# Keys of the first tile in two steps, two more tiles turned on TensorE, and a new written-out order, in a two-layer linear-attention and gated-MLP kernel

## The chip, the cores and the metric

One core of one Trainium2 chip runs the whole program in one launch. The metric is the device time of one execution in microseconds; lower is better. PE is TensorE's matmul stream and PEld its weight loads, DVE is VectorE, ACT is ScalarE, POOL is GpSimd, SP is the engine whose queue issues most of the DMAs.

## The reference

The input x has 2048 rows (tokens) of 512 in bf16. Two layers follow each other; both use the same weights. Each layer adds an attention step and then an MLP step to x, each on a layernorm of x:

```python
def _A_ref(x, wqkv, w_phi, wo):            # H = 32 heads of Dh = 16
    q, k, v = ...                          # from x @ wqkv, split by heads
    pq = einsum("bhsd,hdf->bhsf", q, w_phi)
    pk = einsum("bhsd,hdf->bhsf", k, w_phi)
    phi_q = concat([softmax(pq), softmax(-pq)])
    phi_k = concat([softmax(pk), softmax(-pk)])
    kv = einsum("bhsf,bhsd->bhfd", phi_k, v)
    z  = einsum("bhsf->bhf", phi_k)
    num = einsum("bhqf,bhfd->bhqd", phi_q, kv)
    den = einsum("bhqf,bhf->bhq", phi_q, z) + 1e-6
    return (num / den) @ wo
def _B_ref(x, W_gate, W_up, W_down):       # F = 1376
    gate = x @ W_gate; up = x @ W_up
    return (gate * (gate > 0) * up) @ W_down

x = x + _A_ref(layernorm(x)); x = x + _B_ref(layernorm(x))   # and once more
```

The attention is linear: kv and z are sums over all tokens, so that no query of a layer can be finished before the last key of that layer.

## The kernel before

The tokens are 16 tiles of 128 rows. For each tile of a layer the work is, in order:

- `norm_A`: mean and variance of the tile (DVE, "stats" and "aggr"), `ln` and `rstd` on ACT (rsA), then x scaled to xn (on DVE, or on POOL, there with a small instruction for the negated mean nm before it).
- `turn`: xn is transposed into xnTA. One way is by PE: four transposes of 128 columns against the identity into a PSUM bank, then a copy out by ACT or DVE. The other is one DMA on SP's queue for two tiles at once ("pair"). In the first layer tiles below `PAIRN` go by PE, the others by DMA as pairs; `PAIRN` is 4 before.
- Keys: `Keys.begin` multiplies xnTA with Wk2, takes two exponentials (ek, on ACT, of the value and of its negative), multiplies xnTA with wv (V), copies V into vext, and sums ek on DVE (sk). `finish` and `scale` turn the sums into a factor (ln and exp on ACT) and scale ek in two halves (DVE or POOL). `kvz` adds ek times vext into one PSUM bank over all 16 tiles.
- Queries: `query` multiplies xnTA with Wq2, takes exponentials and sums, scales, and turns the result by DMA (fq).
- `build` makes R from the sums; `attend` multiplies fq with R (erq), divides, turns (oT), and projects with wo; `mlp` does the gated MLP for blocks of one to four tiles.

Wk2 and Wq2 are folded weights: `fold` multiplies the weight with `Wblk`, the block-diagonal form of w_phi with its mean taken off, so that one matmul gives k times w_phi. For that the weight must be turned first: wk by PE (16 transposes of 128 columns into four PSUM banks, copied out to SBUF by ACT or DVE), then for each of four row blocks four matmuls of 128 columns with Wblk (16 in all), and four copies into Wk2. Wq's weight is turned by four DMAs on SP, its 16 fold matmuls go between the first tiles. So a tile's first key needs wk, w_phi (wf), Wblk and all four copies of Wk2; wk lies in a tile that is named hT in the traces, because the MLP uses it later.

Every step is an `op(engine, cost, due, emit, ...)`. The list of ops is made by the loops above; then `arrange` takes each op's order, buffer and engine from written-out tables: `ORDER` is the order of emission (an op's number is its place of creation), `SLOTS` the buffer that each op takes, `PLACE` one digit for each op that has an alternative engine. Each engine runs its instructions in that order and waits at the first that isn't ready. There are six PSUM banks (p_b) for nearly everything on PE and one more for kvz and erq. PE begins with nine matmuls on zeros ("warm"), which compute nothing.

DMA issues share eight semaphores in turn, so that the ninth issue waits for the first to land, the tenth for the second, and so on.

Of the kernel before, what the change touches and what calls it, by code (L numbers as in the profile page):

```python
# [8 lines left out]
P = 128  # L9
# [4 lines left out]
NB = D // P  # L14
NF = 11
FR = F - (NF - 1) * P
T = 16
# [82 lines left out]
def mm(n, cols):  # L100
    t = n * (cols / 2.4 + 2.5)
    return t, t + 170, n
# [40 lines left out]
class K:  # L143
# [9 lines left out]
    "0101111100101100001010011011110000100001111011010110111000001101011001000010110000111010010000010000"  # L153
    "0010010100000001111001111010110011000001111000110110011110001111000101001001000110110000100010000111"
    "0011010011011011000001110101110010000101010010000001001000100010001000001010110001101101010111000011"
    "010000110000000001101011110100010011100001110011101111"
)
SLOTS = (
    "0011542321002200002341032141012103362101231434404125j4422i5312281024c0330125132k00002b0004951314g423"
    "1e41205354370055313a222d131f04582546001b163h300034130124130c2521320706391100050401151502000225011020"  # L160
    "0500001114010022350210003100001155021002001401004000015205125e33102414110214302510310g04000200200152"
    "2215403520252225221j21311041130411310211252130152021002440102353051383314b2000464022f043001410305001"
    "301310400211321121324501222511005434101040159521003032121131131255132033021422h2124c2012020032050152"
    "0422331141155k313015i13215200i034a242k351d265e115d120f13360053054504583237263j2122131a30010401021414"
    "0000124402100044010001340210124302000043011021240110400025211311121001130410105001200503212211011001"
    "3525524313500042000002141022155020245231052132214003203540112501511114520122403101512101402105022135"
    "000200110411442140220243214113013120412210500400541032135"
# [7 lines left out]
PAIRN, PAIRK, READY = 4, T, (2, 3)  # L175
# [100 lines left out]
def kernel(  # L276
    ctx: ExitStack, tc: tile.TileContext, A_x, A_wqkv, A_w_phi, A_wo, B_x, B_W_gate, B_W_up,
    B_W_down, out):
    nc = tc.nc
# [529 lines left out]
    xT = []  # L809
# [101 lines left out]
```

## Time and profile before

| | us |
|---|---|
| median of 3 runs | 373.67 (373.5 to 373.74) |
| the profiled execution's own time | 373.55 |
| its span | 371.8 |
| PE busy | 363.0 (98%) |
| DVE busy | 266.9 (72%) |
| ACT busy | 209.3 (56%) |
| POOL busy | 99.8 (27%) |

A row of a timeline gives the start, the length, the engine and line, the operation with its shapes, how many of them in a row, and in brackets the idle time before it and what ended it. Matmuls are pipelined: one of 512 columns shows as 379 ns though the next starts 216 ns later, so that times on PE are best taken from start to start. A row of the DMA view gives the issue, its size and the time from issue to landing. Shares of busy time are means over stages with different limits.

### The profile page before, as it was taken

How to read it: one execution, taken by the hardware profiler on the slowest of the kernel's cores; microseconds unless marked ns; L12 is line 12 of the kernel's file. 1: busy time of each engine (PE TensorE's matmuls, PEld its weight loads, DVE VectorE, ACT ScalarE, POOL GpSimd, SP SyncE). 2: the span in 40 equal slices, each digit the busy share in tenths (PEclk: the TensorE clock that was granted, in tenths of full speed). 3: DMA queues.
4: the chain of work that ended last, by engine and by line, in shares of the span. 5: the costliest groups of instructions: out<-in, count | busy, mean ns of one | idle time of the engine just before them, and what ended most of it. 6: DMA issues, size and time to landing. Idle time of an engine off the chain costs nothing.

```text
span 371.8 us, 7423 instructions
## 1 busy us (share of the span) xinstructions
PE 363.0 (98%) x2786; PEld 216.4 (58%) x2828; DVE 266.9 (72%) x562; ACT 209.3 (56%) x575; POOL 99.8 (27%) x126
## 2 busy tenths in 40 slices
PE   8899999999999999999999999999999999999996
PEld 4445557776555545455567555687664544457764
DVE  6899999999797573846899887998668362433343
ACT  5989999473644772454554768775343426313111
POOL 4799863350220100003621184252100000000000
PEclk9999999999999999999999999999999999999999
DMA  8869838777516050131134000359754302010033
GB/s 220 190 153 193 278 84 154 112 146 144 111 23 119 2 100 2 29 71 37 28 65 85 3 0 3 58 94 170 151 77 72 51 14 30 0 43 15 9 118 104
DMA packets 93443, 31.20 MB, mean 84 GB/s; under 512 B 85376, under 2 KB 92384, under 8 KB 93408
## 3 DMA queue, kind: packets, MB, share of 16 engines
q1 hardware_dynamic: 92736, 30.59, 40.5%
q8 instruction: 22, 0.36, 0.4%
q10 hardware_dynamic: 672, 0.15, 0.2%
q14 instruction: 13, 0.11, 0.1%
HBM read 7.91 MB, written 2.10 MB: 27 GB/s over the span
## 4 chain that ended last, share of the span: by engine, by line
PE 91%; DMA 3%; ACT 2%; DVE 2%; issue 1%; POOL 0%; DVEq 0%; POOLq 0%
PE b L754 36%; PE b L794 19%; PE b L617 7%; PE b L561 7%; PE b L555 6%; PE b L677 6%; PE b L730 3%; PE q L590 2%; PE q L654 2%; DMA xnTB<-xn 1%; DMA xnTA<-xn 1%; PE q L430 1%; PE b L480 1%; ACT ek L558 1%; DVE X L681 1%
## 5 line engine op out<-in xcount | busy, mean ns | idle before, releaser
L754 PE MATMUL b<-xnTB,wgu 128*128 128x128 bf16 (+2 forms) x1200 | 153.3, 279 | 0.3 <-DMA xnTB<-xn 0.3
L754 PEld LDWEIGHTS <-wgu 128*128 128x128 bf16 x1200 | 97.6, 98 | 47.5 <-DMA xnTB<-xn 0.4
L758 ACT ACTIVATE gu<-b 128x512 bf16<-128x512 f32 (+1 forms) x83 | 47.1, 580 | 70.3 <-PE b L754 64.6
L794 PE MATMUL b<-wd,hT 128*128 128x512 bf16 (+3 forms) x346 | 84.5, 372 | 0.8
L529 POOL TENSOR_TENSOR ek<-ek,sk 128x512 bf16<-128x512 bf16 x47 | 51.2, 1115 | 93.3 <-ACT sk L578 93.3
L794 PEld LDWEIGHTS <-hT 128*128 128x128 bf16 (+1 forms) x363 | 34.3, 98 | 34.1 <-DVE hT L762 0.3
L771 DVE TENSOR_TENSOR hT<-gu,b 128x512 bf16<-128x512 bf16 (+1 forms) x40 | 26.0, 657 | 24.8 <-ACT gu L758 18.7
L566 DVE TENSOR_REDUCE sk<-ek 128x64 f32<-128x1024 bf16 x32 | 38.1, 1207 | 7.9 <-ACT ek L558 7.8
L623 DVE TENSOR_REDUCE sq<-ek 128x64 f32<-128x1024 bf16 x32 | 38.5, 1209 | 6.2 <-ACT ek L620 6.2
L558 ACT ACTIVATE ek<-b 128x512 bf16<-128x512 f32 x64 | 36.4, 607 | 10.0 <-PE b L555 9.0
L638 POOL TENSOR_TENSOR ek<-ek,sq 128x512 bf16<-128x512 bf16 x28 | 30.5, 1094 | 34.5 <-DVE sq L634 23.6
L620 ACT ACTIVATE ek<-b 128x512 bf16<-128x512 f32 x64 | 36.5, 608 | 3.7 <-PE b L617 3.7
L801 DVE SCALAR_TENSOR_TENSOR X<-b,rsB,X 128x512 bf16<-128x512 f32 (+2 forms) x33 | 23.7, 729 | 20.4 <-PE b L794 20.4
L677 PE MATMUL b<-wo,oT 128*128 128x512 bf16 x121 | 32.1, 379 | 0.4
L555 PE MATMUL b<-Wk,xnTA 128*128 128x512 bf16 x119 | 31.2, 379 | 1.3 <-DMA xnTA<-xn 0.8
L561 PE MATMUL b<-wv,xnTA 128*128 128x512 bf16 x128 | 32.2, 379 | 0.1
L773 ACT CAST gu<-b 128x512 bf16<-128x512 f32 (+1 forms) x43 | 24.6, 575 | 13.5 <-PE b L754 10.8
L617 PE MATMUL b<-Wq,xnTA 128*128 128x512 bf16 x119 | 30.7, 379 | 0.3
L762 DVE TENSOR_TENSOR hT<-gu 128x512 bf16<-128x512 bf16 (+1 forms) x43 | 21.7, 511 | 11.9 <-ACT gu L773 11.9
L681 DVE SCALAR_TENSOR_TENSOR X<-b,X 128x512 bf16<-128x512 f32 x32 | 21.7, 683 | 9.5 <-PE b L677 9.1
L668 DVE TENSOR_TENSOR o<-q,rd 128x512 bf16<-128x512 f32 x32 | 22.0, 688 | 3.2 <-ACT rd L665 2.6
L490 DVE BATCH_NORM_STATS2 bstA<-X 128x6 f32<-128x512 bf16 x32 | 21.7, 685 | 2.9 <-DMA X<-in_A_x_dram 2.6
(80 smaller groups left out, 349.1 us busy)
## 6 DMA issues: line engine op xcount, KB each, us to landing
out_dram<-X SPq DMA_DIRECT2D x15, 128.0 KB, 1.8
X<-in_A_x_dram SPq DMA_DIRECT2D x6, 256.0 KB, 4.1
wgu<-in_B_W_up_dram SPq DMA_DIRECT2D x4, 344.0 KB, 4.5
wgu<-in_B_W_gate_dram SPq DMA_DIRECT2D x4, 344.0 KB, 4.7
wd<-in_B_W_down_dram SPq DMA_DIRECT2D x5, 256.0 KB, 5.5
hT<-in_A_wqkv_dram SPq DMA_DIRECT2D x2, 256.0 KB, 3.8
wv<-in_A_wqkv_dram SPq DMA_DIRECT2D x2, 256.0 KB, 4.4
wo<-in_A_wo_dram SPq DMA_DIRECT2D x4, 128.0 KB, 4.2
```

Source lines behind the costliest of these rows:

```text
L529: e.tensor_tensor(out=out().rearrange("p g s (h f) -> p (g s h) f", f=DH)[:, lo:lo + n], in0=ek.t[:].rearrange("p g s (h f) -> p (g s h) f ...
L555: k = op("PE", mm(4, 512), due, lambda: [nc.tensor.matmul(kp.t[:], lhsT=xnTA[c][:, i, b, :], rhs=Wk2[:, b, :], start=(b == 0), stop=(b == ...
L558: e = [op("ACT", act(512), due, lambda s=s: nc.scalar.activation(out=ek.t[:, :, s, :], in_=kp.t[:].rearrange("p (g e) -> p g e", e=GQ), fu ...
L561: v = op("PE", mm(4, 512), due_v, lambda: [nc.tensor.matmul(vp.t[:], lhsT=xnTA[c][:, i, b, :], rhs=wv[:, b, :], start=(b == 0), stop=(b == ...
L566: a = op("DVE", SUM16, due, lambda: nc.vector.tensor_reduce(out=sk.t[:, row, :], in_=ek.t[:].rearrange("p g s (h f) -> p (g s h) f", f=DH) ...
L617: q = op("PE", mm(4, 512), due, lambda: [nc.tensor.matmul(qp.t[:], lhsT=xnTA[c][:, i, b, :], rhs=Wq2[:, b, :], start=(b == 0), stop=(b == ...
L620: e = [op("ACT", act(512), due, lambda s=s: nc.scalar.activation(out=ek.t[:, :, s, :], in_=qp.t[:].rearrange("p (g e) -> p g e", e=GQ), fu ...
L623: a = op("DVE", SUM16, due, lambda: nc.vector.tensor_reduce(out=sq.t[:], in_=ek.t[:].rearrange("p g s (h f) -> p (g s h) f", f=DH), axis=A ...
L677: a = op("PE", mm(4, 512), due + 3, lambda j=j, yp=yp: [nc.tensor.matmul(yp.t[:], lhsT=oT.t[:, j, b, :], rhs=wo[:, b, :], start=(b == 0), ...
L754: nc.tensor.matmul(ps.t[:, q * W:(q + 1) * W].rearrange("p (i t) -> p i t", t=P), lhsT=wgu[:, s, b, g * P:(g + 1) * P], rhs=xT.t[:, 0:n, b ...
L758: nc.scalar.activation(out=gu.t[:, 0, 0:cols], in_=gp.t[:, 0:cols], func=AF.Relu)
L794: nc.tensor.matmul(yp.t[:, 0:c1 - c0], lhsT=h.t[:m, f * W + i * P:f * W + (i + 1) * P], rhs=wd[:m, f, c0:c1], start=(f == 0), stop=(f == N ...
```

## The change

Three things change.

First, tile 0's keys in the first layer no longer use Wk2. With `PLAIN = 1`, the tile's xnTA is multiplied by wk itself as it was loaded: 16 matmuls of 128 columns give the keys in turned form (name "KT"), one copy brings them from PSUM to SBUF (kT, in a buffer of the pool gu), and four matmuls of 128 columns with Wblk give what Wk2 gave. So this tile waits for wk and Wblk but not for the turned wk, its folds and the four copies. The other tiles use Wk2 as before.

Second, `PAIRN` goes from 4 to 6: tiles 4 and 5 of the first layer are turned on PE, each by four transposes and a copy, no longer by a DMA as a pair, and their ln and rsA are taken for each by itself.

Third, `ORDER`, `SLOTS` and `PLACE` are new tables. The op numbers shift by seven, as there are seven more ops. From about the 890th of 1,888 entries the order is the old one but for small swaps. In the first part much moves:

- SP's queue before begins: first half of wk, tiles 2 and 1 of x, second half of wk, tiles 8 and 9, tile 3, a turned block of Wq, tiles 4 and 5, half of wv, tiles 6 and 7, half of wv, three turned blocks of Wq, the turned pair 4 and 5. After it begins: wf (before on ACT's queue), tile 2, wk's two halves, tile 3, tiles 4 and 5, tiles 12 and 13, wv's two halves, tiles 8 and 9, a turned block of Wq, tiles 6 and 7, tile 1, a turned block, tiles 10 and 11, two turned blocks, the turned pair 12 and 13.
- PE before turns all of wk with the first folds between, then tiles 0 to 3, and begins the keys of three tiles. After it turns half of wk, tile 0, a quarter of wk, does a fold, the last quarter, a fold, KT, two folds, turns two tiles, does the second step of tile 0's keys, the values of two tiles, a fold of Wq, and then the first key by Wk2. The first key of a tile turned by DMA (tile 12) comes after eight groups of K and V by 512 columns and all folds of Wq.
- By `PLACE`, in the first part: one Wq copy and one copy of the turned wk go from DVE to ACT, the kT copy is on ACT, three of the copies of turned tiles go to DVE; tile 0's scaling goes from POOL to DVE; in the phi halves two go from POOL to DVE; three of the reciprocals of `attend` go from ACT (as ln and exp) to DVE.

```diff
@@ -150,21 +150,21 @@
 PLACE = (
-    "0101111100101100001010011011110000100001111011010110111000001101011001000010110000111010010000010000"
...
+    "0100100000101001000110111111111000110001101100000010110110100001100111000100110110110101000000000000"
...
 SLOTS = (
...
@@ -172,103 +172,104 @@
 SUM_ON_PE, SPLIT = False, False
-PAIRN, PAIRK, READY = 4, T, (2, 3)
+PAIRN, PAIRK, READY = 6, T, (2, 3)
+PLAIN = 1
...
 ORDER = (
-    16, 0, 3, 17, 30, 22, 24, 25, 8, 4, 26, 18, 19, 7, 1, 12, 47, 9, 323, 27, 48, 31, 28, 20, 2, 49, 33, 83, 50, 10,
...
+    16, 0, 4, 17, 30, 23, 18, 8, 19, 24, 20, 26, 22, 3, 21, 1, 9, 47, 10, 27, 48, 14, 85, 28, 2, 49, 50, 6, 31, 86, 51,
...
@@ -552,9 +553,20 @@
             c, i = t // C, t % C
             kp, vp = Buf(p_a), Buf(p_b)
             ek, vx = Buf(p_ek), Buf(p_v)
-            k = op("PE", mm(4, 512), due, lambda: [nc.tensor.matmul(
-                kp.t[:], lhsT=xnTA[c][:, i, b, :], rhs=Wk2[:, b, :], start=(b == 0), stop=(b == NB - 1))
-                for b in range(NB)], [xT] + k_fold, [kp], name="K")
+            if self.l == 0 and t < PLAIN:
+                kT, tp = Buf(p_gu), Buf(p_b)
+                k = op("PE", (960, 1130, 16), due, lambda: [nc.tensor.matmul(
+                    tp.t[:, e * P:(e + 1) * P], lhsT=wk[:, b, e * P:(e + 1) * P], rhs=xnTA[c][:, i, b, :],
+                    start=(b == 0), stop=(b == NB - 1)) for e in range(NB) for b in range(NB)],
+                    [xT] + l_wk, [tp], name="KT")
+                k = evac("DVE", due, lambda: kT.t[:, 0, :], lambda: tp.t[:], [k], [kT], [tp], "kT")
+                k = op("PE", mm(4, 128), due, lambda: [nc.tensor.matmul(
+                    kp.t[:, b * P:(b + 1) * P], lhsT=kT.t[:, 0, b * P:(b + 1) * P], rhs=Wblk[:, b, :],
+                    start=True, stop=True) for b in range(NB)], [k, c_blk], [kp], [kT], name="K")
+            else:
+                k = op("PE", mm(4, 512), due, lambda: [nc.tensor.matmul(
+                    kp.t[:], lhsT=xnTA[c][:, i, b, :], rhs=Wk2[:, b, :], start=(b == 0), stop=(b == NB - 1))
+                    for b in range(NB)], [xT] + k_fold, [kp], name="K")
```

More of the change, by code (lines that the diff above doesn't have):

```diff
@@ L152 @@
 PLACE = (
-    "0101111100101100001010011011110000100001111011010110111000001101011001000010110000111010010000010000"
-    "0010010100000001111001111010110011000001111000110110011110001111000101001001000110110000100010000111"
-    "0011010011011011000001110101110010000101010010000001001000100010001000001010110001101101010111000011"
-    "010000110000000001101011110100010011100001110011101111"
+    "0100100000101001000110111111111000110001101100000010110110100001100111000100110110110101000000000000"
@@ L157 @@
+    "1010001100011000100100000011010110110000001111000010000011010001111001011100001010110110000100010000"
+    "1110011010011011011000001110101110010000101010010000001001000100010001000001010110001101101010111000"
+    "011010000110000000001101011110100010011100001110011101111"
 )
 SLOTS = (
-    "0011542321002200002341032141012103362101231434404125j4422i5312281024c0330125132k00002b0004951314g423"
-    "1e41205354370055313a222d131f04582546001b163h300034130124130c2521320706391100050401151502000225011020"
@@ L161 @@
[L161 to L165, printed above, removed]
@@ L166 @@
-    "3525524313500042000002141022155020245231052132214003203540112501511114520122403101512101402105022135"
-    "000200110411442140220243214113013120412210500400541032135"
+    "000135042302101020000338141155200220314111214223023342022e0001g23115b4402a53312j2020i013226311554320"
+    "3d5211c01210442490047113f121k234h34111555260e30463302061c211814343550024a002321000305011313020002240"
+    "110201200001153000020340210121000101133020000220504002102521300513d24102511115211211103402b130100002"
+    "2023013021253105114g3230740201251110321242511231001431230421552030231230212405541125e5134h1322005101"
@@ new lines @@
+    "0320012010252240011001021532041430012362301013103332018212114111012013302422224051424035441010400210"
+    "310342541220050033j20220390432i0449135f264j350k203d113k121h132e043c055i0631322a2027214g130f340115200"
+    "2051500101055020002550110012502001052021002520100214501025001031012110111100225020030001013224044011"
+    "1112123133152023211510210041500440332411531202340241052121123510113013100153110145220203040205240231"
+    "14023120400000500551052442452115112212011504400300520350121023"
```

178 rows, old and new, of the table ORDER are left out of this document.

## The prediction

> **What bounds the kernel now.** I read the page's busy line first, then the stretches (busy time by window), then PE's timeline of the first 22 us, then ACT, POOL and the DMA issues beside it.
>
> ```profile
> PE 363.0 (98%) x2786; PEld 216.4 (58%) x2828; DVE 266.9 (72%) x562; ACT 209.3 (56%) x575; POOL 99.8 (27%) x126
> 5.03:18.47 13.44, 11.85 (x97) 7.09 (x96) 12.25 (x32) 12.52 (x37) 10.20 (x20) 1.00 0.90 217
> 18.47:54.00 35.53, 35.20 (x271) 18.33 (x278) 34.63 (x50) 34.15 (x101) 30.77 (x35) 1.00 0.76 182
> 54.00:100.00 46.00, 45.63 (x469) 32.05 (x473) 43.99 (x95) 29.07 (x94) 14.19 (x21) 1.00 0.71 132
> 20.00:30.00 10.00, 9.95 (x61) 4.80 (x61) 10.00 (x19) 9.97 (x30) 9.38 (x13) 1.00 0.67 173
> ```
>
> The columns are length, then PE, PEld, DVE, ACT and POOL busy. PE is the bound of the whole: after 18.47 it is idle for 0.33 us of 35.53, then 0.37 of 46. Only the start loses. So any change to this kernel is worth two things: PE work added, and PE time lost before 18.47. But between 18.47 and 54 ACT and DVE are nearly as full as PE, so that work put on them there has no idle time to go into.
>
> PE's timeline of the start (start, length, line, count, idle before):
>
> ```profile
> 1.19 4.02 PE L430 MATMUL q<-zero 128*128 128x512 bf16 x9 [1.19 <-DVE zero L397]
> 5.00 1.06 PE L454 MATMUL b<-ident,hT 128*128 128x128 bf16 x8
> 6.35 0.79 PE L462 MATMUL b<-Wblk,hT 128*128 128x128 bf16 x8 [0.29 <-POOL Wblk L416]
> 6.97 0.61 PE L454 MATMUL b<-ident,hT 128*128 128x128 bf16 x8
> 9.45 0.40 PE L480 MATMUL b<-ident,xn 128*128 128x128 bf16 x4 [0.40 <-POOL xn L512]
> 9.69 2.75 PE L555 MATMUL b<-Wk,xnTA 128*128 128x512 bf16 x11
> 14.23 0.39 PE L462 MATMUL b<-Wblk,hT 128*128 128x128 bf16 x4
> 14.45 1.03 PE L561 MATMUL b<-wv,xnTA 128*128 128x512 bf16 x4
> 17.30 0.39 PE L462 MATMUL b<-Wblk,hT 128*128 128x128 bf16 x4
> 18.47 1.90 PE L555 MATMUL b<-Wk,xnTA 128*128 128x512 bf16 x7 [0.78 <-DMA xnTA<-xn]
> 20.20 1.03 PE L561 MATMUL b<-wv,xnTA 128*128 128x512 bf16 x4
> 21.07 1.03 PE L617 MATMUL b<-Wq,xnTA 128*128 128x512 bf16 x4
> ```
>
> Lengths overlap, so I price by starts. Four matmuls of 512 columns take 21.07 - 20.20 = 0.87; four of 128 columns 14.45 - 14.23 = 0.22. From the end of the nine warm-up matmuls (5.03) to 18.47 the order of before runs 64 matmuls of 128 columns (16 to turn wk, 16 folds of Wk, 16 folds of Wq, four tiles turned by four) and 32 of 512 (K and V four times each): 16 x 0.22 + 8 x 0.87 = 10.5 us of work in 13.44. So the start loses 2.9 us, the last piece of it in the wait for the first pair of tiles turned by DMA. The new order must take more from these 2.9 us than the change adds.
>
> **PE work added.** Tile 0's K was four matmuls of 512 (0.87). It becomes sixteen of 128 with the plain wk and four of 128 with Wblk: 5 x 0.22 = 1.10, so 0.23 more. Tiles 4 and 5 turned on PE are eight of 128: 0.44. Together 0.67 us, and none of it is hidden unless PE would otherwise wait, which it does only in the start.
>
> **The new start, step by step.** The rows that price it:
>
> ```profile
> 4.68 0.22 DVE L411 TENSOR_REDUCE cmean<-wf 128x4 f32<-128x64 bf16 x1 [0.54 <-DMA wf<-in_A_w_phi_dram]
> 5.25 1.05 POOL L416 TENSOR_TENSOR Wblk<-wf,Mf 128x512 bf16<-128x512 bf16 x1 [3.94 <-DVE vext L399]
> 8.62 0.77 POOL L512 TENSOR_SCALAR xn<-X,nm,rsA 128x512 bf16<-128x512 bf16 x1
> 9.37 0.19 POOL L510 TENSOR_SCALAR nm<-mvA 128x1 f32<-128x1 f32 x1
> 11.91 0.32 ACT L498 ACTIVATE lnA<-mvA,eps 128x2 f32<-128x2 f32 x1
> 12.36 1.07 ACT L558 ACTIVATE ek<-b 128x512 bf16<-128x512 f32 x2
> 13.32 0.30 ACT L498 ACTIVATE lnA<-mvA,eps 128x2 f32<-128x2 f32 x1
> 7.92 1.54 ACT L436 CAST Wk<-b 128x512 bf16<-128x512 f32 x3
> 9.34 0.32 ACT L498 ACTIVATE lnA<-mvA,eps 128x1 f32<-128x1 f32 x1
> 10.95 1.09 ACT L558 ACTIVATE ek<-b 128x512 bf16<-128x512 f32 x2
> wf<-in_A_w_phi_dram ACTq DMA_DIRECT2D x1, 16.0 KB, 3.5
> hT<-in_A_wqkv_dram SPq DMA_DIRECT2D x1, 256.0 KB, 3.3
> hT<-in_A_wqkv_dram SPq DMA_DIRECT2D x1, 256.0 KB, 4.3
> 0.74 0.44 SPq L348 DMA_DIRECT2D hT<-in_A_wqkv_dram  x1
> 7.25 3.81 SPq L449 DMA_TRANSPOSE hT<-in_A_wqkv_dram  x3
> ```
>
> An ACT pass over 512 columns costs 0.48 (two ek from 12.36 to 13.32, three casts from 7.92 to 9.34), an ln with its rsA 0.45 (11.91 to 12.36), a tile scaled on POOL 1.04 (xn at 8.62, its successor's nm at 9.37 and 0.29 more).
>
> Loads. On SP's queue wf now goes first (0.74) and the first half of wk third, behind wf and one tile of x: at somewhat under 0.5 an issue, at about 1.7 rather than 0.74. wf lands 0.74 + 3.5 = 4.24 instead of 4.68, so Wblk is ready near 5.85 instead of 6.30. wk's first half lands at 1.7 + 3.3 = 5.0 at best, and at 1.7 + 4.3 = 6.0 at worst. Bytes queued ahead of it are fewer than ahead of the 4.3 row, so I take 5.1: PE's first turn starts about where it does now.
>
> Tile 0. Its scaling moves from POOL, where it stands behind Wblk, to DVE: statistics, one ln and rsA, and the scaled tile is there near 5.8. PE turns it behind the first eight of wk (until about 6.4), ACT copies it by 7.1, the sixteen matmuls with wk run until about 8.1. ACT must then finish two casts before kT, so the second step runs near 9.1, 0.6 earlier than PE's first K now (9.69).
>
> ACT, the chain that decides. From 8.0 on its new queue holds four casts (Wk, kT, Wk, Wk: 1.9), two ln and two rsA (0.6, half overlapped), a fourth Wk cast, a vext, an ln: tile 0's first exp stands at 8.0 + 1.9 + 0.6 + 0.96 + 0.2 = 11.7, where now it runs at 10.95. So the two-step key does not bring tile 0's exponentials forward; it only gives PE work while ACT is busy. Up to the next wait on a DMA there follow on ACT rsA, vext, three ek, ln, ek, ln, rsA, Wq, rsA, ek, Wq, a key sum's ln, vext, ek: with that first exp eleven passes of 0.48 and 0.9 of small ones, to 17.9. The bank for PE's first K of a DMA-turned tile (tile 12) is then free: PE reaches it at 18.05.
>
> POOL and the pair. POOL scales tiles 2 and 3, then 4 and 5, then the pair 12 and 13. Tile 4 needs an rsA that stands behind those four casts (10.6); the four end at 10.6 + 0.77 + 3 x 1.04 = 14.5. SP is free by then: the transposes of Wq's weights take 1.27 of issue each, and a later start and the loads between them move the last one's end from 11.1 to about 12.3. So the pair is issued at about 14.5, against 13.57 now for the first pair. Its landing:
>
> ```profile
> 13.57 1.23 SPq L475 DMA_TRANSPOSE xnTA<-xn  x1
> xnTA<-xn SPq DMA_TRANSPOSE x1, 4.9
> xnTA<-xn SPq DMA_TRANSPOSE x1, 4.6
> xnTA<-xn SPq DMA_TRANSPOSE x1, 3.4
> X<-in_A_x_dram SPq DMA_DIRECT2D x1, 256.0 KB, 4.1
> ```
>
> These are the first three pairs of before (issued at 13.57, 16.05, 19.17) and a load of x beside the first. The new pair has loads issued right behind it, like the first two, so I take 4.6: landed at 19.1, with 17.9 and 19.4 as ends. The load row is for a transfer of the same 256 KB. The Trainium skill ("Advanced Engine Details and Errata", X-Bar Transpose) says that transposing DMAs are as fast as regular ones; two of three rows here are slower than that load, one faster. By that rule the pair would land at 14.5 + 4.1 = 18.6 and the result would be 0.5 lower than mine.
>
> Sum. Up to this wait the new order has run 88 matmuls of 128 (16 turning wk, five tiles, 16 + 16 folds, 20 for tile 0's K) and 32 of 512: 22 x 0.22 + 8 x 0.87 = 11.8. From 5.03 to 19.1 are 14.07, so the start loses 2.3 against 2.9: 0.6 won. PE's added work takes 0.67. Net +0.07 us, which is nothing. The ends: landing at 17.9 leaves PE's own arrival, 18.05, a loss of 1.2, and the net is 1.7 - 0.67 = 1.0 won; landing at 19.4 gives 2.6 and 0.4 lost.
>
> Behind the start. The order written out is the same but for a shifted numbering and small swaps in its later half, so what counts is 19 to 54. There PE has no slack and I cost the new order at nothing. The cover is ACT's lead: K's and Q's exponentials lag PE by banks. If that cover is gone, see the second rival. DVE gets three more copies of turned tiles, one scaling and two halves of phi, and gives up a Wq cast and a copy of wk's turned weights; the copies stand in its start, where it has 1.2 us idle (13.44 - 12.25). POOL is relieved of a tile and two halves. Of the moved work, one pair fewer on SP (1.23 of issue) frees a queue that nobody waits for.
>
> Against the profiled execution: 373.55 for a span of 371.8, and the median 373.67. 373.55 + 0.07 is 373.6, which I give as the time.
>
> **The rivals.** A measurement of this kernel can tell about 0.2%, 0.75 us, from no change.
>
> Faster: the pair lands like the third one (3.4) and PE never waits; then 1.0 us comes off, 372.6. For it: nothing else is in the transposing queue then. Against it: the two pairs with the same neighbours took 4.6 and 4.9. It can hardly give more, since PE's own arrival hangs on ACT. Chance 0.27.
>
> Slower, by ACT: by the new order's list ACT gets one Wq cast, the kT cast and one more copy of wk's turned weights, one xnTA copy less, and one ln with rsA more (two singles for one pair): 2 x 0.48 + 0.45 = 1.4 us before 54, while it has 1.4 us idle there now (35.53 - 34.15), 0.91 of it one gap:
>
> ```profile
> 19.54 1.09 ACT L558 ACTIVATE ek<-b 128x512 bf16<-128x512 f32 x2 [0.91 <-remote]
> ```
>
> That line is where ACT waited for the keys of the first pair. It decides as soon as PE waits for a bank between 20 and 50: then the 1.4 us arrive on PE whole, 373.6 + 1.4 = 375.0. Against it: three pairs of ln and exp for the denominators go to DVE near 55. Chance 0.22.
>
> Slower, by a late full rate: nine 512-column matmuls of the warm-up took 4.02, 0.43 each against 0.22 later, and the first eight of 128 took 1.06 against 0.61 for the second eight, though the granted clock reads 1.00 throughout. So the array runs at half rate until about 6. If PE pauses for wk at 5.03 and the half rate lasts until 9, the ten groups of 128 that stand between (2.2 us) take 4.4, of which 0.8 falls into waits; ACT, POOL and the pair come 1.4 later: 375.0. The Trainium skill ("TensorE: Matmul & The Clock Gate", Parts 1 and 4) has the array at half rate until some 3.4 us of sustained work and does not count transposes as work, and the new order puts sixteen of them ahead of its first fold where before has eight. The trace agrees on the half rate; that transposes don't count it does not show. Chance 0.08.
>
> Nothing of the start is won: the new start loses 2.9 as the old one does, and only the added work remains, 374.3. Chance 0.10; it is no change by the bound.
>
> **How the numbers follow.** The forecast has 0.33. No change within 0.2% is 372.92 to 374.42: 0.33 + 0.10 = 0.43. Faster 0.27, slower 0.22 + 0.08 = 0.30. The forecast's own range is 372.9 to 374.1. The range to hold 8 in 10 goes from 372.5 to 375.0: it takes in the faster case and the ACT case, and leaves out mixes of the two slower cases.
>
> **What would show it.** Right: tile 0's second step near 9.1, tile 0's first ek near 11.7, the first xnTA pair issued near 14.5, and PE idle 0.5 to 1.4 us before the K that follows, the only DMA wait on PE up to 54. Wrong: the first turn of wk starting after 5.6; PE waiting for banks (idle ended by ACT) between 20 and 54; PE past that K by 18.2; or a PE busy sum that grew by other than 0.7.

## The result, and the profile after

| | before | after |
|---|---|---|
| median of 6 runs, us | 373.47 (373.21 to 373.74) | 375.81 (374.99 to 376.04) |
| the profiled execution's own time | 373.55 | 376.04 |
| its span | 371.8 | 374.2 |
| its last matmul starts | 368.05 | 370.61 |

The change makes the kernel slower: the ratio of the times is 1.006 [1.005, 1.007], 2.3 us. The prediction was 373.6 in 372.5 to 375.0; the time lies above the range.

Busy time by stretch in the changed kernel (length, then PE, PEld, DVE, ACT, POOL, granted clock, DMA share, GB/s):

```profile
5.03:18.47 13.44, 11.94 (x114) 7.70 (x115) 11.76 (x28) 12.01 (x35) 8.06 (x19) 1.00 0.96 223
18.47:54.00 35.53, 35.36 (x283) 18.54 (x282) 35.09 (x46) 35.02 (x105) 32.33 (x35) 1.00 0.69 175
54.00:100.00 46.00, 44.97 (x475) 31.71 (x474) 39.94 (x96) 27.11 (x83) 12.87 (x18) 1.00 0.72 129
```

Against the same rows of before, the start and the stretch up to 54 look no worse. PE's idle time between 54 and 100 has grown from 0.37 to 1.03. DVE's idle time between 18.47 and 54 has shrunk from 0.90 to 0.44. What PE waited for (total, times, longest):

```profile
PE b L567 <- DMA xnTA<-xn: 1.3, 1, 1.3
PE q L431 <- DVE zero L398: 1.2, 1, 1.2
PE b L573 <- DMA wv<-in_A_wqkv_dram: 0.9, 1, 0.9
PE b L455 <- POOL nm L511: 0.8, 1, 0.8
PE q L666 <- DVE R L619: 0.6, 1, 0.6
PE b L481 <- DVE o L680: 0.3, 1, 0.3
PE b L573 <- ACT ek L632: 0.2, 1, 0.2
```

The wait for zero opens the warm-up, as before. The row with nm is the first turn of the key weights, at 5.52; what it waited for is rather their first half, which landed at 5.47. The first line is the largest new one, and PE's timeline puts it in the second layer, in a part of the order that the change left as it was:

```profile
10.58 1.90 PE L573 MATMUL b<-wv,xnTA 128*128 128x512 bf16 x8 [0.94 <-DMA wv<-in_A_wqkv_dram]
55.38 0.41 PE L666 MATMUL q<-R,fq 128*128 128x68 bf16 x8 [0.63 <-DVE R L619]
56.97 0.40 PE L481 MATMUL b<-ident,o 128*128 128x128 bf16 x4 [0.31 <-DVE o L680]
206.88 1.90 PE L567 MATMUL b<-Wk,xnTA 128*128 128x512 bf16 x8 [1.29 <-DMA xnTA<-xn]
```

To find all of the 2.56 us by which the last matmul starts later, I took the start of each matmul in the trace and subtracted what the matmuls before it cost back to back (512 columns 0.216 us, 256 0.109, 128 0.056). In the trace of before 42 matmul records are missing, each put in at its cost. What is left over is time lost:

| stretch, us | lost before | lost after | difference |
|---|---|---|---|
| 1.5 to 30 | 4.86 | 3.91 | -0.95 |
| 30 to 54 | 0.20 | 0.31 | +0.11 |
| 54 to 60 | 0.08 | 1.28 | +1.20 |
| 60 to 200 | 0.30 | 0.71 | +0.41 |
| 200 to 250 | -0.08 | 1.59 | +1.67 |
| 250 to 300 | 0.66 | 0.08 | -0.58 |
| work added on PE | | | +0.70 |

The lines add to 2.56. So there are two losses to explain, 1.20 behind the last key product and 1.67 in the second layer, and two gains, 0.95 in the start and 0.58 near 271.

For the second layer, the DMA view in two windows of 3.1 us, each from the issue of the same pair of tiles on. First before, then after:

```profile
q1 hardware_dynamic: 1056, 0.26, 44.1%
xnTA<-xn SPq DMA_TRANSPOSE x1, 3.0
```

```profile
q1 hardware_dynamic: 1046, 0.26, 44.0%
q8 instruction: 1, 0.02, 1.9%
xnTA<-xn SPq DMA_TRANSPOSE x1, 4.6
```

The pair carries the same bytes, but in the changed kernel one packet of the queue "instruction" moves beside it, and the pair lands after 4.6 us instead of 3.0. Over the whole execution that queue moves 22 packets of 16 KB:

```profile
q8 instruction: 22, 0.36, 0.4%
```

PE runs 2852 matmuls and as many weight loads, so one packet goes with some 260 of its instructions. The packets' times in the trace follow PE's program: 60 empty instructions on PE move the one at 208.5 to 202.7 (e1, below). The change adds 24 pairs of weight load and matmul near the start. The work at 202 us thus moved by 1.5 us, and the packet, counted in pairs, came earlier against it: 208.5 us before, 7.8 behind the issue of this pair; 204.7 after, 2.5 behind it. The theory, then, is that the packet in its flight makes the pair late, and the first experiments test it. Its rival was that the late landing came of the new order or of chance.

### The profile page after: what moved, and what is told of

Read it like the earlier page. It is cut to its first block, busy times and chain, and to the rows that moved or that the text cites. A ratio compares the mean times of both kernels' runs of the same rounds, so it can differ in the third digit from the quotient of the medians.

```text
span 374.2 us, 7496 instructions
## 1 busy us (share of the span) xinstructions
PE 365.3 (98%) x2852; PEld 216.9 (58%) x2852; DVE 268.7 (72%) x568; ACT 209.8 (56%) x574; POOL 97.2 (26%) x122
## 4 chain that ended last, share of the span: by engine, by line
PE 79%; ACT 9%; DVE 6%; DMA 3%; issue 1%; SPq 1%; DVEq 0%
PE b L766 35%; PE b L806 19%; PE b L689 7%; PE b L629 4%; ACT ek L570 4%; PE b L573 3%; PE b L567 3%; PE b L742 3%; PE q L666 2%; DVE ek L530 2%; DMA X<-in_A_x_dram 1%; ACT ek L632 1%; DVE sk L578 1%; ACT vext L437 1%; DMA xnTA<-xn 1%
## 5 line engine op out<-in xcount | busy, mean ns | idle before, releaser
L806 PE MATMUL b<-wd,hT 128*128 128x512 bf16 (+3 forms) x363 | 86.2, 373 | 0.0
L530 POOL TENSOR_TENSOR ek<-ek,sk 128x512 bf16<-128x512 bf16 x45 | 50.3, 1140 | 56.4 <-ACT sk L590 55.2
L570 ACT ACTIVATE ek<-b 128x512 bf16<-128x512 f32 x64 | 36.4, 621 | 7.5 <-PE b L567 7.5
L632 ACT ACTIVATE ek<-b 128x512 bf16<-128x512 f32 x64 | 35.5, 615 | 6.7 <-PE b L629 6.7
L629 PE MATMUL b<-Wq,xnTA 128*128 128x512 bf16 x128 | 32.2, 379 | 0.0
L774 DVE TENSOR_TENSOR hT<-gu 128x512 bf16<-128x512 bf16 (+1 forms) x43 | 20.6, 484 | 12.0 <-ACT gu L785 12.0
```

Source lines behind the costliest of these rows:

```text
L530: e.tensor_tensor(out=out().rearrange("p g s (h f) -> p (g s h) f", f=DH)[:, lo:lo + n], in0=ek.t[:].rearrange("p g s (h f) -> p (g s h) f ...
L570: e = [op("ACT", act(512), due, lambda s=s: nc.scalar.activation(out=ek.t[:, :, s, :], in_=kp.t[:].rearrange("p (g e) -> p g e", e=GQ), fu ...
L629: q = op("PE", mm(4, 512), due, lambda: [nc.tensor.matmul(qp.t[:], lhsT=xnTA[c][:, i, b, :], rhs=Wq2[:, b, :], start=(b == 0), stop=(b == ...
L632: e = [op("ACT", act(512), due, lambda s=s: nc.scalar.activation(out=ek.t[:, :, s, :], in_=qp.t[:].rearrange("p (g e) -> p g e", e=GQ), fu ...
L806: nc.tensor.matmul(yp.t[:, 0:c1 - c0], lhsT=h.t[:m, f * W + i * P:f * W + (i + 1) * P], rhs=wd[:m, f, c0:c1], start=(f == 0), stop=(f == N ...
```

## The experiments

Each was measured against the kernel before on the same chip; the runs were spread over four chips, on which the kernel before took 373.52 to 373.61. e6, e8, e11 and e12 carry e2's empty instructions too, and e7, e8 and e9 some of their own, to keep the packets where they do no harm. The last two columns come from the profiled execution: when PE's first numerator product starts (it needs R, so it stands for everything up to R), and how long PE takes from there to its last matmul.

| run | median, us | ratio to before | first numerator | from there to the end |
|---|---|---|---|---|
| before | 373.47 | | 53.85 | 314.20 |
| after | 375.81 | 1.006 [1.005, 1.007] | 55.38 | 315.23 |
| e1_shift_before | 375.47 | 1.0045 [1.0033, 1.0057] | 53.81 | 316.46 |
| e2_shift_after | 373.95 | 1.0012 [1.0003, 1.0021] | 55.39 | 313.74 |
| e3_cover | 376.00 | 1.0065 [1.0053, 1.0077] | 55.01 | 315.48 |
| e4_both | 374.04 | 1.0017 [1.0004, 1.0030] | 57.39 | 313.84 |
| e5_before_clear | 372.94 | 0.9987 [0.9978, 0.9996] | 53.70 | 313.74 |
| e6_mask_early | 373.35 | 1.0003 [0.9990, 1.0016] | 54.89 | 313.38 |
| e7_pair_by_dma | 379.31 | 1.0143 [1.0126, 1.0161] | 59.92 | 314.09 |
| e8_one_step_keys | 374.77 | 1.0041 [1.0024, 1.0057] | 56.02 | 313.41 |
| e9_turn_alone | 373.21 | 0.9991 [0.9982, 1.0000] | 54.02 | 313.72 |
| e10_before_clear2 | 373.37 | 0.9995 [0.9986, 1.0004] | 54.17 | 313.79 |
| e11_ek_early | 374.36 | 1.0029 [1.0017, 1.0042] | 55.23 | 313.49 |
| e12_ek_and_mask | 373.74 | 1.0004 [0.9995, 1.0012] | 54.80 | 313.52 |

**e1 and e2: move the packet, nothing else.** The means is an empty instruction on PE. It does no work, but it takes a place in PE's program, so that every packet behind it comes earlier against the work. Before and after get a few of them where PE's sequencer runs ahead of the array:

```diff
             if o.eng == "PE":
                 idle(next(fill, 0))
             o.emit()
+            if o.eng == "PE":
+                for _ in range(NOPS.get(pe, 0)):
+                    nc.tensor.nop("pad")
+                pe += 1
+NOPS = {k: 6 for k in range(256, 266)}     # e1, in the kernel before
+NOPS = {k: 7 for k in range(256, 266)}     # e2, in the changed kernel
```

> The kernel before with 60 empty instructions in TensorE's program, six behind each of ten of its steps between about 190 and 197 us, so that its instruction packet of 16 KB that moved at 208.5 us comes 30 pairs of weight load and matmul earlier, at about 203. Theory 1 (such a packet that falls into the flight of a transposing DMA lengthens it): the pair issued near 200.7 us lands after 4.6 to 4.9 us and not 3.04, its K waits about 1.3 us near 205.5, and the time is 374.4 to 375.0 against 373.5. Theory 2 (the late landing in the changed kernel comes of its other order, or of chance): the pair lands after about 3.05 us and the time stays 373.4 to 373.7. If the empty instructions themselves cost, TensorE shows gaps between 190 and 197 us; expected is under 0.2 us.

> The changed kernel with 70 empty instructions in TensorE's program, seven behind each of ten of its steps between about 189 and 197 us, so that its instruction packet that moved at 204.7 us comes 35 pairs earlier, at about 200.4, ahead of the pair that is issued at 202.2. Theory 1 (packet in the flight lengthens it): that pair lands after about 3.05 us and not 4.63, the wait of 1.3 us at 206.9 is gone, and the time is 374.4 to 374.8 against 375.8. Theory 2: the pair still lands after 4.6 us, and the time stays at 375.8, or rises by what the empty instructions cost.

The DMA view over 3.1 us from the issue of the pair, in e1 (the kernel before with the packet moved into the flight):

```profile
q8 instruction: 1, 0.02, 1.8%
xnTA<-xn SPq DMA_TRANSPOSE x1, 4.4
```

and in e2 (the changed kernel with the packet moved out of it; no such line of the queue is there):

```profile
q1 hardware_dynamic: 1056, 0.26, 44.1%
xnTA<-xn SPq DMA_TRANSPOSE x1, 3.1
```

The same edit makes the one kernel slower by 1.95 and the other faster by 1.86. In e2 the wait is gone and PE loses 0.13 between 200 and 250 instead of 1.59. In e1 PE waits where it never did, and at a second place, which the expectation did not have:

```profile
205.11 1.25 PE L555 MATMUL b<-Wk,xnTA 128*128 128x512 bf16 x5 [1.03 <-DMA xnTA<-xn]
287.02 1.04 PE L677 MATMUL b<-wo,oT 128*128 128x512 bf16 x4 [1.35 <-ACT gu L773]
```

The second is again a packet (at 282.7) in the flight of a pair of oT, issued at 281.67, that landed after 5.3 us; the row names ACT, which had long been done. Both kernels' gaps between 190 and 200 us stayed as they were, so the empty instructions cost nothing there. Theory 1 stands: the landings came as it had them, in both directions. The times went further than it had them, e1 over its 375.0 by the second place, and e2 under its 374.4: of e2's 1.86 the profiled executions show 1.5, and for the rest I have no place.

**e3 and e4: give PE something to do while it waits for R.** Two Q groups move ahead, on PE alone:

```diff
- PE's part of ORDER: ... Q470, erq488, Q443, oT492, erq496, Q407 ...
+ PE's part of ORDER: ... Q470, Q443, erq488, Q407, oT492, erq496 ...
```

> The changed kernel with two steps of its written-out order moved on TensorE alone: the Q group that stood behind the first numerator product now stands ahead of it, and the next Q group stands ahead of the first turn of o. Theory 1 (the 1.2 us that TensorE loses between 54 and 60 us is the wait for R on VectorE with too little to do meanwhile): the waits of 0.63 for R and 0.31 for o shrink to 0.2 together, and the time falls by 0.6 to 1.1 us, to 374.7 to 375.2. Theory 2 (VectorE and ScalarE are late by as much in what follows, and the wait only moves): the gaps reappear between 57 and 75 us, and the time stays within 0.3 us of 375.8.

> The changed kernel with both edits, the two Q groups moved and the 70 empty instructions. If the two losses are separate, the gains add: 1.0 to 1.4 for the packet and 0.6 to 1.1 for the cover, 373.3 to 374.2 us, level with the kernel before (373.5) within 0.7. If the new order loses by something else as well, or the cover is given back, it stays over 374.4.

In e3 the wait for R is gone, and two others stand in its place, behind R in the same chain:

```profile
56.60 0.40 PE L481 MATMUL b<-ident,o 128*128 128x128 bf16 x4 [0.31 <-DVE o L680]
57.68 1.04 PE L689 MATMUL b<-wo,oT 128*128 128x512 bf16 x4 [0.42 <-ACT oT L437]
```

PE lost 1.27 us between 54 and 60, against 1.28. e4, with the packet cleared as well, is 0.1 from e2, which lacks the move, so that its 374.04 lies in the range for two gains by the packet's alone. Theory 2 had the time and the waits behind R right: a Q group moved ahead fills the wait for R and is then missing in the chain from R to the first projection. e4's profiled execution took 376.66, 2.6 over its median; the last section says why.

**e6, e11 and e12: why R is late.** VectorE around R (start, length, operation) before, and after:

```profile
49.03 0.57 DVE L424 TENSOR_TENSOR Mg<-Mf 128x4 f32<-128x4 f32 x1
53.01 0.69 DVE L602 TENSOR_TENSOR R<-q,Mg 128x512 bf16<-128x512 f32 x1 [0.29 <-PE q L590]
53.71 1.21 DVE L623 TENSOR_REDUCE sq<-ek 128x64 f32<-128x1024 bf16 x1
```

```profile
52.49 1.01 DVE L425 TENSOR_TENSOR Mg<-Mf 128x4 f32<-128x4 f32 x1
53.43 1.21 DVE L635 TENSOR_REDUCE sq<-ek 128x64 f32<-128x1024 bf16 x1
54.55 0.67 DVE L614 TENSOR_TENSOR R<-q,Mg 128x512 bf16<-128x512 f32 x1
```

Before, VectorE stands idle when the last key product ends (52.97) and takes R at once. After, it has no idle time: the last key product ends at 53.88, and a sum that stands behind the mask keeps VectorE until R at 54.55. So R is 1.55 later: 0.91 because PE itself comes to its last key product later, with one Q group (0.87) more ahead of it, and 0.64 on VectorE, which takes 0.67 from there to R where it took 0.04. e6 moves the mask to where VectorE waits for x. Each line shows the part of one engine, VectorE for the mask and ScalarE for ek:

```diff
 ORDER: ... 38, 121 (stats), 260 ...   ->  ... 38, 121, 29 (Mg), 260 ...      # e6, e12
 ORDER: ... 42 (W2), 142 (ln) ...      ->  ... 42, 57, 58 (ek of tile 0), 142 ...   # e11, e12
```

> The changed kernel with the 70 empty instructions of the run before (packet clear of the pair at 202 us) and one VectorE step moved in the written-out order: the 1.0 us that spreads the mask Mg, which stood two steps ahead of R at 52.5 us, goes to 8.3 us, where VectorE waits for x. Theory 1 (the 1.2 us between 54 and 60 us come of VectorE, which is 2.2 us behind with Mg and a sum when the last key product ends): R starts at about 53.9 and not 54.55, what TensorE loses there falls from 1.28 to 0.2 to 0.5 us, and the time is 372.9 to 373.4 against 373.95 without the move. Theory 2 (the chain behind R is as late as R, as moving Q groups showed, so the loss moves on): 373.7 to 374.1.

> The changed kernel with the 70 empty instructions that clear the pair at 202 us, and one move on ScalarE in the written-out order: tile 0's two exponentials, which stood behind the value copy and began at 12.5 us, stand right behind the third copy of the folded weights, at about 9.9, where ScalarE waited 0.77 us. In every run so far R started 41.4 to 42.2 us after the first exponential of keys, with ScalarE busy for 97 to 99 per cent of that and VectorE for 99. Theory A (ScalarE's stream sets R): R starts 0.5 to 0.8 us earlier than 54.55, and the time is 373.1 to 373.5 against 373.95 without the move. Theory B (VectorE's stream sets R): R stays within 0.2 of 54.55, and the time at 373.8 to 374.1.

> The run beside it with the mask Mg moved to 8.3 us on VectorE as well. Theory A alone: as the run beside it, 373.1 to 373.5. Theory B alone: as the mask alone, R at about 54.05 and 373.2 to 373.5. Both streams near their bound: R at 53.3 to 53.7, what TensorE loses between 54 and 60 us falls under 0.5, and the time is 372.5 to 373.1, under the kernel before.

VectorE in e6:

```profile
52.63 1.21 DVE L635 TENSOR_REDUCE sq<-ek 128x64 f32<-128x1024 bf16 x1
54.05 0.69 DVE L614 TENSOR_TENSOR R<-q,Mg 128x512 bf16<-128x512 f32 x1 [0.22 <-PE q L602]
```

VectorE is now ahead of the last key product, which ends at 54.01, and waits 0.22 for it. R starts 0.5 earlier, PE's loss between 54 and 60 falls from 1.28 to 0.65, and the time from 373.95 to 373.35. The time lies in Theory 1's range; the loss does not, it was to fall to 0.2 to 0.5. Theory 1 had VectorE 2.2 behind, and it was 0.67. What is left lies behind R, where the wait of 0.31 for o stays. (The intervals of the ratios of e2 and e6 overlap, so that the 0.6 of time is less sure than the rows.) In e11 tile 0's first exponential starts at 9.91 instead of 12.53, and R comes no earlier than this:

```profile
54.41 0.67 DVE L614 TENSOR_TENSOR R<-q,Mg 128x512 bf16<-128x512 f32 x1
```

R is 0.15 earlier than in e2, within the 0.2 of Theory B. So ScalarE's stream does not set R, and Theory A falls. The regularity that had led me to it (42 us from the first exponential to R in nearly every run) was a coincidence of starts: in e11 it is 44.5. e12 repeats e6 (R at 53.96). The medians of e11 and e12 are each 0.4 above the kernel without the earlier exponentials (374.36 against e2's 373.95, 373.74 against e6's 373.35), above the ranges of both theories, and I have no place for that: the profiled execution of e11 took less than that of e2 (374.19, 374.58).

**e5 and e10: clear the packets in the kernel before.** Empty instructions only, dealt out in two ways (in short):

```diff
+NOPS = {0: 42, and 5 behind each of ten steps at 211 to 220 us}     # e5
+NOPS = {0: 36, and 6 or 5 behind each of the same ten}              # e10
```

> The kernel before, nothing of its work changed, with 42 empty instructions behind its warm-up products, where TensorE waits for weights anyway, and 50 more in ten of its steps between about 211 and 220 us. Its packets of 16 KB of instructions then come 21 pairs of weight load and matmul earlier (the one at 16.4 us at about 13.2), and 46 pairs earlier from 220 us on (the one at 269.4 at about 262.5). Theory 1 (a packet in the flight lengthens a transposing DMA): the first pair of normalised tiles, issued at 13.6 us, lands after 3.1 to 3.5 us and not 4.85, the wait of 0.7 to 0.8 us at 18.5 is gone, so is that of 0.3 at 271.5, and the time is 372.2 to 372.8 against 373.5. What the change won at its start would then be had without the change. Theory 2 (those landings are late for another reason, as the loads of x and of the weights beside them): they stay, and the time is 373.4 to 373.6. A packet that falls on another pair that is waited for would cost 0.3 to 1.5 us, at a place that the waits name.

> The kernel before with the empty instructions of the earlier run dealt out otherwise: 36 behind the warm-up instead of 42, 56 at 211 to 220 us instead of 50. The packet that fell at 33.1 us into the flight of the pair issued at 30.2 (4.87 us, a wait of 0.6 us at 35.2) then comes at about 34, into the flight of the pair behind it, which landed after 6 us in the kernel before without a wait. Theory 1: the wait at 35.2 is gone and none comes in its place, 372.1 to 372.5. Theory 2 (that wait has another cause): it stays, 372.9.

In the kernel before, the first pair had been issued at 13.57 and had landed after 4.9 us, with a packet at 16.4. In e5 the packet comes at 12.2, and the pair lands after 3.1; PE's K stands at 17.61 instead of 18.47, without a wait. But a later packet, at 33.1, now falls 2.84 behind the issue of a pair that landed after 3.1 before, and this pair lands after 4.9:

```profile
35.17 1.04 PE L555 MATMUL b<-Wk,xnTA 128*128 128x512 bf16 x4 [0.58 <-DMA xnTA<-xn]
```

With that wait e5 misses its range (372.2 to 372.8) by 0.14. In e10 the wait at 35 is gone as expected, but not because the packet left the flight: at 33.36 it stands 2.84 behind the issue, as in e5, and the pair lands after 3.1 all the same. That late in the flight a packet does not always count (the last section has more such cases). And e10 is slower than e5 and than its own range of 372.1 to 372.5. One of PE's waits in e10:

```profile
PE b L617 <- ACT vext L436: 1.0, 1, 1.0
```

It is at 48.2 us: PE, now 0.8 ahead, runs into a bank that waits for ACT's copy. The first numerator product is at 53.7 and 54.2 in e5 and e10, against 53.85 before. So what PE wins in the start is given back before R: in e5 at 35 us, in e10 at 48. The other gain stays: the wait of 0.3 at 271 us is gone in both. e5 does the same work as the kernel before, and its interval is the only one here that lies wholly under 1.

**e7, e8 and e9: the parts of the change.** One switch each, with ORDER, SLOTS and PLACE to match:

```diff
-PAIRN = 6   +PAIRN = 4    # e7, in the changed kernel: tiles 4 and 5 by DMA, K and V of both later
-PLAIN = 1   +PLAIN = 0    # e8, in the changed kernel: tile 0's K from Wk2, behind the second V
-PAIRN = 4   +PAIRN = 6    # e9, in the kernel before: turns of tiles 4 and 5 behind a fold at 14.2
```

> The changed kernel with one part undone: tiles 4 and 5 again turned as a pair by one transposing DMA, their K and V products moved behind two other steps of the order to give it time; 36 empty instructions behind the warm-up and 50 at 190 to 197 us keep the instruction packets clear of both pairs. TensorE works 0.44 us less, VectorE makes two copies of 0.41 less. The pair should be issued at about 13.4 and land at 16.5, TensorE should be there at about 15.6. Theory 1 (turning on TensorE was worth its 0.44 because TensorE has nothing else to do then): 0.3 to 0.9 us slower than with both on TensorE, 374.2 to 374.9. Theory 2 (the turns and their copies are what made VectorE late at R): the time falls to 373.2 to 373.7, and less is lost between 54 and 60 us.

> The changed kernel with the other part undone: tile 0's keys in one step from the folded weights, made behind the second V product; 32 empty instructions behind the warm-up stand for the 16 matmuls that fall out, so that the instruction packets stay where they were, and the 70 at 189 to 197 us stay. Theory 1 (TensorE's start is bound by the landing of the value weights at about 10.5 us, so the two-step product fills time that is idle otherwise): the step that replaces it adds 0.86 us behind 10.5, and the time is 374.6 to 374.9 against 373.95. Theory 2 (the two-step key costs what it adds, 0.23 us, and nothing waits): 373.6 to 373.8.

> The kernel before with one part of the change alone: tiles 4 and 5 turned on TensorE one by one, behind the product that TensorE reaches at 14.2 us, their copies on VectorE; the order is otherwise that of before, the keys of tile 0 stay in one step. Empty instructions (24 behind the warm-up, 52 at 211 to 220 us) keep the instruction packets off the pairs that are waited for. Against the next kernel, which differs by the turning alone: TensorE works 0.44 us more, VectorE 0.82. Theory 1 (the pair's flight was covered when no packet fell into it, so turning on TensorE only costs): 0.3 to 0.9 us slower than the next kernel, 372.7 to 373.4. Theory 2 (the wait for the pair was the price of the DMA, and turning removes it): level with the next kernel or faster, 372.2 or below.

e8 is 0.82 slower than e2, as Theory 1 had it: the two-step key runs in time that is idle otherwise, before the value weights land. It is worth about 0.8 in this order by the medians, and 0.63 by the start of the first numerator product, although it adds 0.23 of work. e9 is 0.16 under e10 and 0.27 over e5, where one theory had it 0.3 to 0.9 over e10 and the other at 372.2 or below: turning tiles 4 and 5 on PE is worth nothing either way that these runs can tell, its 0.44 of work included, and the same holds for e9 against before. e7, at 379.31 far over both its ranges, says nothing about turning. The places that I gave K and V made PE wait 1.66 us for ACT's copy of Wq, and then the granted clock fell to 0.51, as the second row shows for the stretch from 17.5 to 21 us (the one execution of its four with a mean granted clock of 1.00 took 377.42):

```profile
16.66 1.03 PE L573 MATMUL b<-wv,xnTA 128*128 128x512 bf16 x4 [1.66 <-ACT Wq L437]
17.50:21.00 3.50, 3.50 (x16) 1.83 (x15) 3.50 (x8) 1.39 (x4) 1.54 (x3) 0.51 0.82 230
```

## Why the prediction was wrong, step by step

- **What bounds the kernel: half right.** PE carries the sum, as the table of losses shows. The prediction also saw that ACT and DVE are nearly as full between 18 and 54, but drew the conclusion only for ACT. It costed VectorE's added copies and scaling at nothing, because the start had idle time for them. The idle time that mattered was VectorE's 0.3 us at R. The prediction's list also lacked the dearest single operation that VectorE has more ahead of R, the sum of one more Q group (1.21); which of its additions made it late was not separated.
- **PE work added, 0.67: right.** It is 0.70, from the counts of matmuls by size. PE's busy sums on the two pages (363.0, 365.3) say more, but they don't compare, because of the 42 of 2828 records that are missing in the trace of before.
- **The start, 0.6 won: right in sign, with wrong terms.** It won 0.95. The first half of wk landed at 5.47 (5.1 predicted), and the second key step came at 9.25 (9.1). Not seen was the wait of 0.94 for the value weights at 10.58. Tile 0's first exponential came at 12.53 (11.7), the pair's issue at 15.39 (14.5). The pair's landing, the term on which the sum turned, was taken as 4.6 and was 3.06, and the wait that I expected before its K did not come. The row of 4.9 that I went by had a packet in its flight and landed after 3.1 without it (e5, e10). The row of 4.6 had one 0.34 behind its issue, but in e10 the same pair took 4.5 without any, so that its cause is open. By the Trainium skill ("Advanced Engine Details and Errata", X-Bar Transpose) the pair should land like a regular transfer of its size. It landed faster (3.06) than the loads of 256 KB of x in this kernel (median 4.9).
- **"Behind the start ... I cost the new order at nothing": this is the step that failed.** It cost 0.11 up to 54, 1.20 at R, 0.41 in small gaps up to 200, and 1.67 less 0.58 in the second layer. Of these, the 1.67 is shown to be the packet in the flight of the pair (e1, e2), which is no wait of the new order but a fetch that the 24 added pairs of instructions moved; most of the 0.58 is a wait of before that is gone there too once its packet is cleared (e5, e10). 0.63 of the 1.20 is shown to be VectorE's queue (e6). The other half of the 1.20 and the 0.41 stay open; moving Q groups did not lessen the 1.20 (e3). One more Q group stands ahead of the first numerator product than before (13 against 12), which leaves one less for the chain behind R; that this is the reason was not tried.
- **The faster rival: its condition came true, its gain did not.** The pair landed even earlier than 3.4, and PE did not wait for it. But the start won 0.95 and not the 1.7 that the rival needs: PE waited for the value weights instead. And a gain in the start need not last until R, as e10 shows in the kernel before.
- **Slower by ACT, 375.0: the wrong engine, and not the larger loss.** ACT was as full as forecast (35.02 of 35.53) and made PE wait once, 0.2. That a full engine between 18 and 54 would turn added work into PE's time was right for VectorE.
- **Late full rate: not in the changed kernel's profiled execution,** whose warm-up took 3.50 us instead of 4.02. In e4 and e7 a half rate did come, but as a fall from the full rate behind later waits, not as a late start.
- **The range.** Without the packet's hit the changed kernel takes 373.95, 0.35 above the forecast and inside the range. Even that is in part luck: the 1.20 lost at R, which the prediction had at nothing, is set off by 0.35 more won in the start and by the 0.58 near 271. The mechanism that took the time out of the range was in no rival, although the profile of before held it: pairs issued at 13.57 and 266.57 us that landed after 4.9, each with a packet in its flight. It was not the only cause there, since the latest pair of before, issued at 33.59, landed after 6.1 without a packet.

## What to carry to other kernels

A change that adds or removes instructions on PE moves every later fetch of PE's instructions against the work, and a fetch that met a transfer that PE waited for cost nearly 2 us here (1.95 over two places in e1, 1.86 in e2), twice the 0.95 that the start won. So compare landings of one kind of DMA before pricing one, look for what moved beside the late ones, and test a new wait in untouched code with empty instructions before explaining it by the change. Where three engines are full together, ask of each what it still holds when the hand-over comes (here R), since time won on one of them ahead of that point can be given back before it (e5, e10).

## What the runs showed of the hardware

**A packet of instructions lengthens a transposing DMA that it meets.** I took the fourteen traces behind 100 us, and of the transposing DMAs into xnTA, xnTB, fq and oT those over 2.6 us, which leaves out single tiles (2.4 to 2.6 where no packet meets them; a few that a packet lengthened may be among the late ones). Of 423 with no packet from 1.3 us ahead of their issue to 3.2 behind it, none landed later than 3.7 us. Of 99 with a packet 0.2 to 2.9 behind the issue, 45 took more than 4.0 and up to 5.3 (58 more have a packet nearer the edges and are in neither count). Where the packet fell 0.9 to 2.3 behind the issue, all 26 took 3.66 or more. From 2.3 to 2.9 behind it there is nothing between: 29 took 3.05 to 3.19 and 21 took 4.61 to 5.09. The packet itself takes one of sixteen DMA engines for about 0.94 us (1.9% of 16 engines in the window of 3.1 us), less than the 1.5 that the pair is late. Why it costs more than its own time was not tried. Ahead of 100 us a packet is not the only cause: of 287 without one, 23 landed after more than 3.7, the latest after 6.25 (e1).

**One small operation took 0.17, 0.57 and 1.01 us.** The mask of 4 columns took 0.17 in e6 at 9.3 us, 0.57 before at 49.0 and 1.01 after at 52.5, the last beside a phi half on POOL that took 1.50 instead of its usual 1.06. The Trainium skill ("SBUF — State Buffer", SBUF: two separate sides) has VectorE and GpSimd share a pair of ports as an exclusive lock, which a VectorE operation with two SBUF inputs takes against a GpSimd operation that reads SBUF. The two long cases agree: each ended within 0.02 us of a phi half on POOL (49.59 and 53.48). So does e10, where POOL was idle and the mask took 0.14. The 0.17 was beside POOL's scaling of a tile and does not agree, so the traces do not decide it.

**The clock can fall back for 3.4 us.** The granted clock in e4, behind three waits of PE (0.26, 0.57 and 0.84 us):

```profile
8.00:10.80 2.80, 1.24 (x16) 0.90 (x16) 2.13 (x5) 2.30 (x6) 0.89 (x2) 1.00 1.52 257
10.85:14.24 3.39, 3.39 (x8) 1.20 (x9) 3.39 (x11) 2.55 (x9) 2.05 (x5) 0.50 0.98 262
```

Eight matmuls of 512 columns took 3.4 us instead of 1.7, and this execution took 376.66 where the median of its kernel is 374.04. In e2 two such waits (0.33 and 0.57) and in the changed kernel one of 0.94 at the same step did not do it. It came in e7 as well, and by their mean granted clock (0.994 to 0.995, as in e4's execution) in three of e7's four executions and in one each of e6 and e8, which lie 2.6 and 2.0 us over their medians. The Trainium skill ("TensorE: Matmul & The Clock Gate", Part 1) has the gate judge activity in windows of about 3.4 us that run free of the kernel, which fits the length and that it comes in some executions alone. It has the half rate follow an idle window of that length, and here PE was busy for 1.24 of the 2.80 us ahead, so that the trace does not bear this part out.
